# Lag of layer 2's output matmuls behind its features raised from 15 to 18, and the split of an early weight moved two steps later

## The chip, the cores and the metric

One NeuronCore of one Trainium2 chip runs the whole program. The metric is device time in microseconds (us) of one execution; three executions of the kernel before gave 966.13, 966.22 and 969.75 us, median 966.22.

## What is computed

Random-feature attention (4 x 8 heads, 576 positions, head size 64, 128 features), then two feed-forward layers on its 2304 x 512 result, all in fp32 accuracy:

```python
h = proj - sq; h = h - np.max(h, axis=-1, keepdims=True)
phi = np.exp(h) / np.sqrt(m)                       # of q and of k
num = einsum(q_p, k_p^T v);  den = einsum(q_p, sum k_p) + 1e-6
x = num / den                                      # attention, 2304 x 512
xn = x / rms * rms_g                               # layer 1, d_ff 1536
x = (silu(xn @ w_gate) * (xn @ w_val)) @ w_out
h = x @ w_in                                       # layer 2, d_ff 2048
out = (h * np.cos(h)) @ w_out
```

## The kernel before, in words

**Arithmetic.** A 32-bit operand of a feed-forward product is held as two parts, a high one (a ScalarE cast) and a low one (the difference, on GpSimd or VectorE), and a product is three matmuls: high x high, low x high, high x low. Layer 2's first product, and most of layer 1's, are done by a scheme that needs seven block products instead of eight (`PRODUCTS`).

**Weights (class `Weights`, L129).** A weight chunk of 128 x 512 numbers arrives as 64-bit floats (`load`, L160, a 512 KB transfer) and is made in two generators. `front` (L187) has six steps: (1) a shift on VectorE, (2) for some chunks a sign step on VectorE, (3) a mask on VectorE, (4) `exponent` of the next chunk, an ACTIVATE on ScalarE (L182 or L184) that reads the next chunk's raw tile, (5) a multiply-add on VectorE (L204), (6) the sum on GpSimd (L209). For the twelve early chunks the second generator is `early_back` (L329): its first step is the high cast on ScalarE (L214, `w<-f`) and the issue, on ScalarE's queue, of the load of the raw tile three chunks on; its second step is the low difference on GpSimd (L217). `run` (L314) takes steps of `front(c)` and `early_back(c - 1)` in turn: F1 B1 F2 B2 F3 F4 F5 F6. All engines take their instructions in the order in which this code writes them.

**Attention (L800 to L811).** 24 slots. Each projects one tile of keys or queries (`project`, L419, two PSUM banks of the pool "w", which has four), takes the largest entry on VectorE (L435, `kmx`, `qmx`), and eight exponentials on ScalarE (L437, `ke`, `qe`), four for each bank. Some slots also take a bank of the same pool for a transposition (L502). At the end of a slot `wts.tick` makes weight steps: five in slots 1 to 5, one in slots 6 to 13, four in slots 14 to 22. Eight steps make a chunk, so a chunk is two slots late in the stage.

**Layer 2 (L1182 to L1396).** 24 periods k: three pairs of token blocks by eight groups of two feature tiles. A period has seven `hidden(k, i)` products (six matmuls of 384 columns, L1043, banks `Xh` and `Yh`), each read out by a ScalarE copy (L1196; i = 0, 2, 3, 6) or a VectorE addition (L1199; i = 1, 4, 5). The next product into the same bank, two products on, waits for that. `cosine` (L1210) turns the sums into features: range reduction on VectorE (L1220, L1221), two ScalarE functions (L1017), a product on VectorE (L1232), a high cast on ScalarE (L1051) and a low difference on VectorE (L1054, `o<-turns,o`). `out2(k)` (L1236) is the output product of period k: 36 matmuls of 512 columns (L1251, `o_ps`), four slots of nine (three row blocks by three parts); they are written between the hidden products, `share[i]` of them behind product i. The list for k = 1 opens with fewer, and what it leaves out is the lag: 21 of 36 at k = 1, so 15 are left at each later period's start and run at its head. After each hidden product and after each share, `unit()` runs what is due: features, evictions, weight steps (1.3 back steps a unit), transfers.

A run is a stretch of periods with the same pair; its outputs stay in six PSUM banks and are evicted (L1282 a ScalarE copy, L1276 a VectorE addition) at matmuls 21, 24, 27, 30, 33 and 36 of the run's last `out2`. Runs open at k = 0, 3, 6, 12, 15, 20 and 22. Twenty weight tiles rotate (`RING`); `room` (L360) stops the back steps until `freed_by(k - 1)` (L1346) has told that the tiles of an earlier period have been read. Followed through the code, `room` stops the back steps of layer 2 only until the calls in periods 7 and 16; after the first the tiles of the second group follow one another at fixed distances (a chunk asked from memory is used eight units later), after the second those of the third.

Of the kernel before, what the change touches and what calls it, by code (L numbers as in the profile page):

```python
# [56 lines left out]
def attention_then_ffn(ctx: ExitStack, tc: tile.TileContext, qT, kT, v, omT, wc1, rms_g, wc2, out, B, H, S, D):  # L57
# [69 lines left out]
    class Weights:  # L127
# [186 lines left out]
        def run(self):  # L314

            self.exponent(0)
            yield
            for c in range(self.fused + 1):
                both = [self.front(c)] if c < self.fused else []
                if c > 0:  # L320
                    both.append(self.early_back(c - 1))
                while both:
                    for g in list(both):
                        if next(g, DONE) is DONE:
                            both.remove(g)
                        else:
                            yield
# [217 lines left out]
    with tc.manual_schedule():  # L545
# [467 lines left out]
        def unit():  # L1013
            now = due.setdefault(clock[0], [])
            while now:
                f, args = now.pop(0)
                f(*args)  # L1017
            del due[clock[0]]
            flush(1)
            wts.now += 1  # L1020
            wts.pace(*tempo)
            job(2 if clock[0] % 5 < 2 else 1)
            clock[0] += 1
# [150 lines left out]
        begins_run = [k == 0 or ends_run[k - 1] for k in range(NPER)]  # L1174
# [7 lines left out]
        def hidden(k, i):  # L1182

            n, g, p, fq = periods[k]
            f = 2 * fq
            which, name, acc = PRODUCTS[i]
            if i == 0:
                for x in "XY" if k % 2 == 0 else "YX":
                    banks2[k, x] = bank("wa", f"{x}h_{k}")[:, :NB]
            o = banks2[k, acc]  # L1190
            seventh(o, 2, p, f, which, name, i in (0, 1, 3))
            if i in (0, 2, 3, 6):
                if i in (2, 6) or (k, i) == (0, 0):
                    rows2[k + (i > 2), i // 2 % 3] = two_rows(F32, f"h{i}_{k}")
                a = rows2[k, 1][:, 3 - i] if i in (2, 3) else rows2[k + (i > 2), 0][:, int(i == 0)]
                nc.scalar.copy(a, o)  # L1196
            else:
                a = rows2[k, int(i > 1)][:, (1, 0, 1)[(1, 4, 5).index(i)]]
                nc.vector.tensor_tensor(a, o, a, op=ALU.add)  # L1199
            if i == 1:  # L1200
                cosine(k, rows2.pop((k, 0)), ([(k - 1, 2 * periods[k - 1][3] + 1, 2 * periods[k - 1][2])] if k else [])
                       + [(k, f, 2 * p)])
            elif k + 1 == NPER and i in (4, 5, 6):
                cosine(k, rows2[k + (i == 6), int(i < 6)], [(k, f + (i != 5), 2 * p + (i < 6))], int(i == 5))
            elif i == 5:
                cosine(k, rows2.pop((k, 1)), [(k, f + 1, 2 * p + 1), (k, f, 2 * p + 1)])
            if ends_run[k] and k + 1 < NPER:
                at(1, bring, 3 + periods[k + 1][1], periods[k + 1][2], name)
# [59 lines left out]
        def ask_sums(k):  # L1268
            for m, (blk, j) in enumerate([(2 * periods[k][2] + 1 - c, j) for c in range(2) for j in range(TPB)]):
                if (blk, j) in spilled:  # L1270
                    at(2 * m, ask_sum, blk, j)
# [74 lines left out]
        def freed_by(k):  # L1346

            n, g, p, fq = periods[k]
            if n + 1 == len(sessions) or sessions[n + 1][0] != g:
                wts.freed = first_tile[g] + sum(PARTS2[:GROUPS2[g].index(fq)]) + 3  # L1350
            elif sessions[n - 1][0] != g and fq == GROUPS2[g][0]:
                wts.freed = first_tile[g]
# [3 lines left out]
        for k in range(1, NPER):  # L1356
            loading = ends_run[k]
            tempo[:] = wts.rate(wts.fused + FRONT_GOALS[k], 14) if k in FRONT_GOALS else 0.0, 0.5 if loading else 1.3
            if ends_run[k - 1]:
                ask_sums(k - 1)  # L1360
            share = [1, 2, 3, 3, 4, 4, 4] if k == 1 else [5, 5, 3, 5, 6, 6, 6] if begins_run[k - 1] else [5, 5, 5, 5, 5, 5, 6]
            for i in range(7):
                if (k, i) == (len(GROUPS2[0]), 4):
                    assert not whole
                    wider.pop()
                    extra.close()
                    outs.append(ctx.enter_context(tc.tile_pool(name="outs", bufs=1, reuse_waits="tile")))
                hidden(k, i)
                unit()
                for _ in range(share[i]):  # L1370
                    next(o)
                unit()
                if i == 2 and k > 1:
                    freed_by(k - 1)
                if (i, k + 1) == (3, NPER):
                    ask_sums(k)
# [53 lines left out]
```

## Time and profile before

| | |
|---|---|
| median of three executions | 966.22 us |
| the profiled execution | 965.95 us, span 964.2 us |
| matmul (PE) busy | 951.0 us, 99% of the span |
| VectorE, ScalarE, GpSimd busy | 710.2, 537.1, 415.5 us |
| granted TensorE clock | 1.00 in the mean |
| DMA | 227.65 MB, mean 236 GB/s |

PE is TensorE's matmul row, DVE VectorE, ACT ScalarE, POOL GpSimd, SP the sync engine's queue. Times in rows are us from the span's start. In a row of a timeline the first number is the start, the second the length; `x16` counts the merged instructions, and the bracket gives idle time of that engine just before and who ended it. A projection or a kv product of four heads and two halves shows as 16 matmul records.

### The profile page before, as it was taken

What the parts mean: (1) busy time and instruction counts of PE and PEld (TensorE: products, weight loads), DVE (VectorE), ACT (ScalarE), POOL (GpSimd) and SP (SyncE); (2) the same over time, 40 slices, a digit from 0 to 9 for tenths busy, and PEclk for the clock granted to TensorE, in tenths of its full rate; (3) what the DMA queues carried; (4) which work ended last, traced back from release to release, by engine and by line L of the source; (5) the groups of instructions that cost most, each with busy time, mean ns of one, the idle gap of its engine ahead of it and who ended that gap; (6) DMA issues with size and microseconds to landing.
All of it is one profiled execution on the core that took longest, in us unless ns stands there. A gap on an engine that the chain in (4) does not pass through costs nothing. (4 is left out here: it accounts for less than half of the span.)

```text
span 964.2 us, 16225 instructions
## 1 busy us (share of the span) xinstructions
PE 951.0 (99%) x5761; PEld 894.6 (93%) x5761; DVE 710.2 (74%) x1163; ACT 537.1 (56%) x1155; POOL 415.5 (43%) x377
## 2 busy tenths in 40 slices
PE   9999999999999999999999999999999999999998
PEld 8998999989999999999999998889889889889997
DVE  5786677778863686577685758996799777785766
ACT  7787776775543524355443545575655565464443
POOL 2133366657944867275764663320244220130000
PEclk9999999999999999999999999999999999999999
DMA  8565187778697898856989794967622768307554
GB/s 311 159 179 186 56 279 277 253 267 261 220 329 289 331 331 290 302 154 196 391 281 370 263 356 142 352 226 262 207 88 85 265 199 293 120 23 264 203 219 166
DMA packets 96082, 227.65 MB, mean 236 GB/s; under 512 B 9728, under 2 KB 45184, under 8 KB 96000
## 3 DMA queue, kind: packets, MB, share of 16 engines
q1 hardware_dynamic: 94704, 222.34, 67.0%
q10 hardware_dynamic: 1296, 4.26, 1.3%
q8 instruction: 46, 0.75, 0.3%
q14 instruction: 36, 0.29, 0.1%
HBM read 156.04 MB, written 70.52 MB: 235 GB/s over the span
## 5 line engine op out<-in xcount | busy, mean ns | idle before, releaser
L1251 PE MATMUL o_ps<-w,o 128*128 128x512 f32 x864 | 225.7, 393 | 0.7 <-DVE o L1054 0.7
L209 POOL TENSOR_TENSOR f<-f,raw 128x512 f32<-128x512 f32 x68 | 94.3, 1387 | 234.9 <-DVE raw L204 205.1
L1251 PEld LDWEIGHTS o_ps<-w,o 128*128 128x128 f32 x864 | 159.6, 188 | 25.0 <-DVE o L1054 1.1
L217 POOL TENSOR_TENSOR w<-b,w 128x512 fp32r<-128x512 f32 x88 | 115.3, 1316 | 136.7 <-ACT w L214 127.0
L831 PE MATMUL gv_ps<-xhl,w 128*128 128x384 f32 x576 | 108.0, 335 | 1.6 <-DVE gv L870 1.1
L831 PEld LDWEIGHTS gv_ps<-xhl,w 128*128 128x128 f32 x576 | 100.6, 188 | 2.2 <-DVE gv L870 1.4
L1150 PE MATMUL y<-t,w 128*128 128x384 f32 x576 | 102.1, 334 | 0.3 <-POOL w L217 0.3
L1150 PEld LDWEIGHTS y<-t,w 128*128 128x128 f32 x576 | 100.0, 188 | 0.6 <-POOL w L217 0.6
L1051 ACT CAST o<-turns 128x384 fp32r<-128x384 f32 x96 | 47.5, 513 | 95.0 <-DVE turns L1232 95.0
L1043 PE MATMUL Xh<-T,w 128*128 128x384 f32 x432 | 88.6, 340 | 1.7 <-ACT h L1196 1.7
L1043 PEld LDWEIGHTS Xh<-T,w 128*128 128x128 f32 x432 | 78.0, 188 | 9.2 <-ACT h L1196 4.0
L1043 PE MATMUL X<-T,w 128*128 128x384 f32 x432 | 80.9, 335 | 0.0
L1043 PEld LDWEIGHTS X<-T,w 128*128 128x128 f32 x432 | 75.3, 188 | 0.3 <-DVE r L1078 0.2
L214 ACT CAST w<-b 128x512 fp32r<-128x512 f32 x88 | 50.5, 580 | 32.2 <-DVE b L274 25.1
L1054 DVE TENSOR_TENSOR o<-turns,o 128x384 fp32r<-128x384 f32 x96 | 59.9, 640 | 8.2 <-ACT o L1051 8.1
L884 PE MATMUL y_ps<-t,w 128*128 128x384 f32 x288 | 60.7, 346 | 0.0
L1043 PE MATMUL Yh<-B,w 128*128 128x384 f32 x288 | 58.7, 338 | 0.0
L1199 DVE TENSOR_TENSOR h<-Yh,h 128x384 f32<-128x384 f32 x48 | 26.6, 553 | 42.4 <-PE Yh L1043 41.5
L1221 DVE SCALAR_TENSOR_TENSOR turns<-turns,r 128x768 f32<-128x768 int32 (+1 forms) x50 | 56.4, 1128 | 1.7
L1017 ACT ACTIVATE turns<-turns,half_pi 128x768 f32<-128x768 f32 (+1 forms) x50 | 45.7, 915 | 21.4 <-DVE turns L1221 21.3
L190 DVE TENSOR_SCALAR f<-W 128x512 int32<-128x512 int32 x68 | 44.8, 658 | 15.2 <-ACT W L182 6.5
L1043 PEld LDWEIGHTS Yh<-B,w 128*128 128x128 f32 x288 | 52.2, 188 | 3.8 <-ACT h L1196 0.2
(117 smaller groups left out, 1882.0 us busy)
## 6 DMA issues: line engine op xcount, KB each, us to landing
T<-T_dram SPq DMA_DIRECT2D x48, 768.0 KB, 7.0
raw<-wc SPq DMA_DIRECT2D x60, 512.0 KB, 4.9
B<-yh_dram SPq DMA_DIRECT2D x21, 768.0 KB, 5.4
kept<-f SPq DMA_DIRECT2D x56, 256.0 KB, 4.8
b<-kept SPq DMA_DIRECT2D x56, 256.0 KB, 4.9
B<-x_dram SPq DMA_DIRECT2D x15, 768.0 KB, 6.9
x_dram<-xhl SPq DMA_DIRECT2D x12, 768.0 KB, 5.8
s<-x_dram SPq DMA_DIRECT2D x24, 384.0 KB, 5.9
```

Source lines behind the costliest of these rows:

```text
L209: nc.gpsimd.tensor_tensor(f32(f), f32(f), rest, op=ALU.add)
L214: nc.scalar.copy(t[:, 0, to], src)
L217: nc.gpsimd.tensor_tensor(t[:, 1, to], src, f32(t[:, 0, to]), op=ALU.subtract)
L831: nc.tensor.matmul(o, w[i], x[j], start=n == 0, stop=n == len(terms) - 1)
L884: nc.tensor.matmul(yacc[blk][e], w[:, i, e * P:(e + 1) * P], t[:, j], start=first and i + j == 0, stop=last and j == 1)
L1017: f(*args)
L1043: nc.tensor.matmul(o, w[:, i, c + kk * P:c + (kk + 1) * P], x[:, j, kk], start=begin and n == 0, stop=n == 5, skip_group_check=True)
L1051: nc.scalar.copy(t[:, 0], a)
L1054: engine.tensor_tensor(t[:, 1], a, f32(t[:, 0]), op=ALU.subtract)
L1150: nc.tensor.matmul(acc[e], w[:, i, e * P:(e + 1) * P], t[:, j], start=f == fs[0] and i + j == 0, stop=f == fs[-1] and j == 1)
L1221: nc.vector.scalar_tensor_tensor(r, a, -TWO_PI_LO, b, op0=ALU.mult, op1=ALU.add)
L1251: nc.tensor.matmul(oacc[blk][j], o[:, x, js], w[:, y], start=first and n == 0, stop=last and n == 2)
```

## The change

Two independent edits. In `run`, `early_back(c - 1)` joins two steps later, so the order of a chunk is F1 F2 F3 B1 F4 B2 F5 F6; no step is added or removed. In layer 2, the list for k = 1 gives 18 matmuls instead of 21, so every later period runs 18 of the previous `out2` before its own follows; `freed_by` is called one product later to match.

```diff
@@ run
             for c in range(self.fused + 1):
                 both = [self.front(c)] if c < self.fused else []
-                if c > 0:
-                    both.append(self.early_back(c - 1))
-                while both:
+                after = [self.early_back(c - 1)] if c > 0 else []
+                n = 0
+                while both or after:
+                    n += 1
+                    if n > 2 or not both:
+                        both += after
+                        after = []
                     for g in list(both):
@@ layer 2
-            share = [1, 2, 3, 3, 4, 4, 4] if k == 1 else [5, 5, 3, 5, 6, 6, 6] if begins_run[k - 1] else [5, 5, 5, 5, 5, 5, 6]
+            share = [0, 1, 2, 3, 3, 4, 5] if k == 1 else [5, 5, 3, 5, 6, 6, 6] if begins_run[k - 1] else [5, 5, 5, 5, 5, 5, 6]
@@
-                if i == 2 and k > 1:
+                if i == 3 and k > 1:
                     freed_by(k - 1)
```

## Rows read from the trace of the kernel before

**Rows 1.** The page, part 1: busy us, share of the span, instructions.

```profile
PE 951.0 (99%) x5761; PEld 894.6 (93%) x5761; DVE 710.2 (74%) x1163; ACT 537.1 (56%) x1155; POOL 415.5 (43%) x377
```

**Rows 2.** Who PE waited for, whole span: us in total, times, longest.

```profile
PE Xh L1043 <- ACT h L1196: 1.7, 3, 1.0
...
PE o_ps L1251 <- DVE o L1054: 0.7, 1, 0.7
```

**Rows 3.** Busy time by window, layer 2's periods 1, 2, 6 and 9 (start:end, length, busy).

```profile
585.15:599.48 14.33, 12.90 (x65) 10.94 (x64) 13.51 (x19) 8.02 (x16) 5.15 (x4) 1.00 0.07 25
599.48:617.03 17.55, 16.34 (x78) 14.00 (x79) 17.12 (x25) 11.47 (x24) 5.04 (x3) 1.00 0.87 285
...
664.64:680.40 15.76, 15.76 (x80) 14.19 (x79) 10.93 (x19) 7.78 (x13) 1.30 (x1) 1.00 0.57 186
...
711.87:727.60 15.73, 15.40 (x77) 13.62 (x76) 15.28 (x20) 9.02 (x17) 7.44 (x6) 1.00 0.31 104
```

**Rows 4.** Chain of work that ended last: the last 57 output matmuls.

```profile
947.55 12.98 PE o_ps L1251 x57
```

**Rows 5.** Timeline of PE, 76 to 86 us, around the project of slot 23.

```profile
82.90 0.48 PE L426 MATMUL qp_ps<-om,qraw 64*128 64x128 f32 x2
84.05 1.16 PE L426 MATMUL qp_ps<-om,qraw 64*128 64x128 f32 x14 [0.66 <-ACT ke L437]
85.13 1.98 PE L464 MATMUL num_ps<-kv,eT 128*64 128x128 f32 x32
```

**Rows 6.** Timelines of ACT, then DVE, slots 21 and 22.

```profile
81.08 0.64 ACT L452 COPY eT<-eT_ps 128x512 f32<-128x512 f32 x1
82.33 0.62 ACT L214 CAST w<-f 128x512 fp32r<-128x512 f32 x1 [0.62 <-POOL f L209]
...
82.86 2.17 ACT L437 ACTIVATE ke<-kp_ps,kmx 128x128 f32<-128x128 f32 x8
...
81.07 1.28 DVE L435 TENSOR_REDUCE kmx<-kp_ps 128x4 f32<-128x512 f32 x2
```

**Rows 7.** DMA view of 0 to 30 us (issues, KB, us to landing); timelines of ACT and PE.

```profile
raw<-wc SPq DMA_DIRECT2D x3, 512.0 KB, 6.8
raw<-wc ACTq DMA_DIRECT2D x3, 512.0 KB, 4.5
...
16.12 2.18 ACT L437 ACTIVATE ke<-kp_ps,kmx 128x128 f32<-128x128 f32 x8
...
21.22 2.29 ACT L437 ACTIVATE ke<-kp_ps,kmx 128x128 f32<-128x128 f32 x8
...
22.43 3.82 PE L587 MATMUL kv_ps<-v,ke 64*128 64x128 f32 x31
```

**Rows 8.** Timeline of PE, periods 1 and 2 of layer 2.

```profile
591.92 1.31 PE L1043 MATMUL Xh<-T,w 128*128 128x384 f32 x6 [0.31 <-ACT h L1196]
...
594.37 0.73 PE L1251 MATMUL o_ps<-w,o 128*128 128x512 f32 x2 [0.67 <-DVE o L1054]
...
599.48 1.31 PE L1043 MATMUL Xh<-B,w 128*128 128x384 f32 x6 [0.44 <-DVE h L1199]
...
610.05 1.31 PE L1043 MATMUL Xh<-T,w 128*128 128x384 f32 x6 [1.03 <-ACT h L1196]
```

**Rows 9.** Timeline of DVE in the same periods.

```profile
592.89 0.96 DVE L1221 SCALAR_TENSOR_TENSOR turns<-turns,r 128x768 f32<-128x768 int32 x1
...
598.88 0.54 DVE L1199 TENSOR_TENSOR h<-Yh,h 128x384 f32<-128x384 f32 x1
...
603.04 1.94 DVE L1221 SCALAR_TENSOR_TENSOR turns<-turns,r 128x768 f32<-128x768 int32 x1
```

**Rows 10.** Timelines of POOL at 600 us and of PE at 721 us.

```profile
600.51 3.65 POOL L217 TENSOR_TENSOR w<-b,w 128x512 fp32r<-128x512 f32 x2 [2.38 <-ACT w L214]
...
721.22 1.33 PE L1043 MATMUL Xh<-T,w 128*128 128x384 f32 x6 [0.33 <-ACT h L1196]
```

**Rows 11.** Costliest groups by line: the evictions of the output banks.

```profile
L1276 DVE TENSOR_TENSOR sum<-o_ps,sum 128x512 f32<-128x512 f32 x24 | 16.0, 685 | 5.3 <-PE o_ps L1251 5.3
```

## Prediction

> **What bounds the kernel now.** The order of views was: the page's busy times, the list of who PE waited for, the windows of layer 2, and then single timelines where PE stood still. The page gives PE 951.0 us busy of a span of 964.2 [rows 1]; neither edit adds or removes a matmul, so only the 13 us that PE isn't busy, and what lies hidden in its row, can change. The list of waits is short: thirteen lines of 1.7 us or less, the largest three copies by ACT of `Xh` and, of interest here, one wait of 0.7 us of an output matmul for its feature [rows 2]. The windows show where layer 2 loses time: period 6 takes 15.76 us with PE busy throughout, period 2 takes 17.55, and in periods 1 and 2 DVE is busy 13.51 of 14.33 and 17.12 of 17.55 us, against 10.93 of 15.76 in period 6 [rows 3]. So the kernel is bound by PE, save in a few places; the two that the edits touch are the start of layer 2, bound by DVE, and slots 20 to 23 of the attention.
>
> The profiled execution took 965.95 us, 0.27 below the median of 966.22; the sum is made against 965.95 and 0.27 is added at the end. A measurement of this kernel can tell about 0.5% (4.8 us) from no change.
>
> **Early weights: the gain.** In slot 23 PE makes two matmuls of a projection at 82.90 and the third only at 84.05; the next fourteen take 85.13 - 84.05 = 1.08 us, 0.077 each, so two should take 0.15 and 84.05 - 82.90 - 0.15 = 1.0 us is lost [rows 5]. The wait is for ACT's exponentials: a transposition took a bank before, so the second bank of this projection is the one that slot 22's first four exponentials read. They run from 82.86, half of 2.17 us, to 83.95. Their input was there early: DVE's maximum of the first bank ended at 81.07 + 0.64 = 81.71, and ACT's copy ahead of them at 81.72. What stands between is one cast of an early weight, which sat at the head of ACT's queue for 0.62 us until GpSimd's sum was made, and then took 0.62 [rows 6]. With the edit this cast is written one slot later, behind those exponentials and just ahead of the ACTIVATE of front step four. In the same way the cast of slot 19 comes to the end of slot 20; it can push slot 21's work on ACT by at most its own 0.62, so the exponentials of slot 22 start between 81.72 and 82.34, and four are done between 82.81 and 83.43, where PE asks at 83.05. That gives back 0.6 to 1.0; I take 0.8, and zero as the other end, if PE finds another wait right behind.
>
> **Early weights: the price.** `early_back` also issues a load on ACT's queue, so each load moves with its cast. From slot 14 on it has a whole chunk (two slots) to land. In the first slots ticks come five at a time: the load of chunk 3 moves from the end of slot 2 to the end of slot 3, while the ACTIVATE that reads it, the fifth step of chunk 2's list instead of the sixth, comes from the end of slot 5 to the end of slot 4, ahead of slot 5's exponentials. Slot 3's exponentials start at 16.12 and take 2.18 [rows 7]; without the cast of 0.62 ahead of them they end at about 17.7, and the load leaves then. Landing takes 4.5 us on this queue and 6.8 on SP's in the same 30 us [rows 7], so the tile is there at 22.2 or 24.5. With an ACTIVATE of about the cast's 0.62 the exponentials of slot 5 start at 22.8 or 25.1 instead of 21.22, and the first four end 1.1 later, at 23.9 or 26.2. PE wants them in the second half of its 31 kv matmuls, at 22.43 + 3.82/2 = 24.3 [rows 7]. So the price is 0 or 1.9; I take 0.2, since 4.5 is the row of the same queue and kind.
>
> The other moved instructions have one answer: the order within DVE's and GpSimd's queues stays as it was among the weight steps, and there are as many ticks, so from the fourth step of layer 1 on the program is the same.
>
> **The lag: periods 1 and 2.** An output matmul takes 12.98/57 = 0.228 us [rows 4]. Period 1 gets 0, 1, 2, 3, 3, 4, 5 in place of 1, 2, 3, 3, 4, 4, 4: three less, 0.68 us of PE work that ends up at the tail, where 54 in place of 51 matmuls follow the last product. Does PE reach the later products sooner in return? It waits at 591.92 for ACT's copy, at 594.37 for the low half of a feature, at 599.48 for DVE's addition, at 610.05 for ACT's copy again [rows 8]. The second wait goes: that matmul, the twelfth, then comes one hidden product later. The others stand in DVE's queue: the addition that 599.48 waits for runs at 598.88 [rows 9], in a window where DVE is busy 94% of the time [rows 3], and it depends on none of the deferred matmuls. PE then only arrives earlier and waits longer: 599.48 and 610.05 stay, and three matmuls fewer lie before them. I take +0.7. The other end is that PE's waits here all go: 14.33 - 12.90 = 1.4 in period 1 and 17.55 - 15.76 = 1.8 in period 2, together -3.2 [rows 3].
>
> **The lag: the room for weight tiles.** `freed_by` comes one product later, two units, 2 x 15.76/14 = 2.3 us. It is what the back steps wait for in periods 7 and 16. The second group's tiles follow one another at fixed distances from there, so their casts, additions and differences in periods 7 to 11 all come 2.3 us later; no tile is due that soon (the tightest, in period 11, is begun eight units, 9 us, ahead of its use, then seven). In period 9 PE stands 0.33 us at 721.22 for ACT's copy [rows 10]; a weight's cast is written just ahead of this copy and moves behind it. I take -0.3. The other end is one slow instruction more on DVE's path: a range reduction takes 0.96 us alone and 1.94 where GpSimd's differences (600.51 to 604.16) run beside it, so +1.0 [rows 9, 10]. By the Trainium skill (page SBUF — State Buffer, section Who interferes with whom) a VectorE instruction with two SBUF inputs and a GpSimd one that reads SBUF exclude each other for the whole of the first. The 1.94 beside 0.96 agrees. That rule speaks against moving the differences, and is the third rival.
>
> **The lag: evictions and tail.** At a run's end the banks are read at matmuls 21 to 36. With 18 left these fall one behind product 0, two behind product 1, one behind 2, and two (33 and 36) behind 3, where the fourth product had one before. VectorE's takes 0.685 [rows 11]. PE needs the addition of product 4 only at product 6, twelve matmuls (2.7 us) and a product later; two evictions take 1.4. So 0, with 6 run ends x 0.685 = 4.1 as the other end. The last six evictions and their transfers stand behind the same matmuls as before: 0.
>
> **Sum.** -0.8 + 0.2 + 0.7 - 0.3 = -0.2: 965.75 for the profiled execution, and with 0.27 **966.0 us**: no difference that can be told.
>
> **Rivals.**
> 1. *The lag frees PE* (0.12). If the waits of periods 1 and 2 hang on outputs being too close to their features, they go: 965.95 - 0.6 - 3.2 - 0.3 + 0.27 = 962.1, and more if later waits go too. For it: the wait at 594.37 is exactly this. Against it: DVE is over 94% busy there.
> 2. *The third raw tile is late* (0.09), on the other side. Place: the end of slot 4, where ACT stands at the ACTIVATE with slot 5's exponentials behind it and PE behind those. It decides from a landing after 22.6 (4.9 us); at 6.8 it costs 1.9 instead of 0.2: 967.7, slower than before.
> 3. *The moved differences meet VectorE's chain* (0.10): +1.0 in place of -0.3 in periods 7 to 11: 967.3.
> 4. *The paired evictions delay the read-out* (0.04): up to 4.1 more, 970.1.
> 5. *The edits don't reach PE* (0.03): the order changes only in work that is hidden, and the gap at 84 us is kept by DVE's maximum: 966.2.
>
> **How the numbers follow.** My forecast has 0.62. From 964.0 (the forecast with half of rival 1's gain) to 968.4 (rivals 2 and 3 together) lie the forecast, rivals 2, 3 and 5, and a part of rival 1; rival 4 and the rest are outside. Faster by over 0.5% (below 961.4) needs more than rival 1's whole 3.2, a third of its chance: 0.04. Slower by over 0.5% (above 971.1) needs rival 4 with another: 0.03. The rest, 0.93, is the same.
>
> **What would show it.** In the profile of the changed kernel: in slot 23 no wait of the projection for ACT (right), or the same 1.0 us with another releaser (wrong); ACT's ACTIVATE in slot 4 waiting for a transfer at about 21 to 22 us, and no gap of PE at 24 to 26; period 1 still some 14.3 us long with 18 output matmuls in it, the wait for a feature gone and longer waits for ACT and DVE in its place. If period 1 shrinks by more than 0.7 us, or period 2 ends earlier by the same count of matmuls, the reading of DVE as the bound there is wrong. If PE shows new waits for DVE behind products 3 to 6 of periods 4, 7, 13, 16, 21 and 23, rival 4 is right. A total outside 964.0 to 968.4 would make the prediction wrong.

## The result and the profile after

The changed kernel takes 976.46 us (median of six executions, 975.78 to 979.74) against 967.25 us for the kernel before beside it: a ratio of 1.0098, 95% interval 1.0079 to 1.0117. It is some 9 us slower, far above the forecast of 966.0 and outside its range. The profiled execution is the longest of the six (979.74 us, span 977.9). Lines of the code behind `run` are four higher than before (L1251 is L1255 now).

The page of the kernel after, the busy times of part 1 and the clock row of part 2; then the list of who PE waited for (total, times, longest, in us):

```profile
PE 958.2 (98%) x5761; PEld 898.9 (92%) x5761; DVE 713.6 (73%) x1163; ACT 536.0 (55%) x1155; POOL 418.2 (43%) x377
...
PEclk9899999999999999999999999999999999999999
```

```profile
PE Xh L1047 <- ACT h L1200: 2.0, 3, 1.0
PE kv_ps L591 <- DVE kv L602: 1.9, 2, 1.3
PE X L1047 <- DVE r L1082: 1.5, 1, 1.5
PE Xh L1047 <- DVE h L1203: 1.3, 3, 0.6
PE qp_ps L430 <- ACT ke L441: 1.3, 1, 1.3
```

The same 5761 matmuls are busy for 958.2 instead of 951.0 us [rows 1]. Waits are not in this number: the digit 8 in the clock row says that TensorE did not have its full clock in the second fortieth of the span. The wait of an output matmul for its feature [rows 2] is gone, as forecast; in its place stand two waits of the attention's kv product, a longer one of a projection (1.3 instead of 0.7), one of layer 1 (`X`, which the last section takes up), and more of layer 2's products.

**Where the time went.** The n-th matmul into a tile of one name is the same matmul in both kernels, so the difference of their starts is a running account. It stands at 0.2 us by 21 us, 1.8 at the first kv product behind 24 us, 5.1 behind this product at 31 us, 5.6 at 66, 6.5 at 77, 7.1 at 91, 8.7 at 96, 9.0 at 143, 10.7 at 370, 11.1 at the end of layer 2's period 2, 12.6 at 752 and 13.4 at the last matmul. Most of it is there before layer 2 begins. The account is 4 us above the difference of the medians, since the profiled execution is the longest: 1.6 us of it stand for a second fall of the clock at 92 us and 1.7 for a wait at 370 us; whether the other five executions have these isn't shown. PE's timeline of the kernel after, at the four steps in the attention:

```profile
24.13 7.25 PE L591 MATMUL kv_ps<-v,ke 64*128 64x128 f32 x32 [1.31 <-DVE kv L602]
...
66.11 1.16 PE L430 MATMUL kp_ps<-om,kraw 64*128 64x128 f32 x14 [0.58 <-ACT ke L441]
...
76.60 4.03 PE L591 MATMUL kv_ps<-v,ke 64*128 64x128 f32 x32 [0.58 <-DVE kv L602]
91.18 1.16 PE L430 MATMUL qp_ps<-om,qraw 64*128 64x128 f32 x14 [1.30 <-ACT ke L441]
```

The first kv product waits for VectorE's copy of the previous one, and then its 32 matmuls take 7.25 us where 31 took 3.82 [rows 7]. The windows of 22 to 32 us of the kernel after (busy times of PE, PEld, DVE, ACT and POOL, granted clock, DMA share, GB/s) say why:

```profile
22.00:24.00 2.00, 0.83 (x15) 0.63 (x11) 1.97 (x6) 1.67 (x6) 1.41 (x1) 1.00 0.80 243
24.00:26.00 2.00, 1.87 (x9) 1.87 (x10) 2.00 (x6) 1.37 (x7) 0.91 (x1) 0.59 0.59 221
26.00:28.00 2.00, 2.00 (x10) 1.78 (x9) 0.88 (x2) 2.00 (x8) 0.49 (x1) 0.50 0.04 12
28.00:30.00 2.00, 2.00 (x11) 2.00 (x11) 0.00 (x0) 0.15 (x1) 0.00 (x0) 0.50 0.50 131
30.00:32.00 2.00, 2.00 (x19) 1.84 (x20) 0.00 (x0) 0.00 (x0) 0.00 (x0) 0.70 0.00 0
```

PE is busy for 0.83 of the 2 us from 22 to 24, and then the granted clock is 0.50, the lower of the two levels (1.2 GHz), where the kernel before has 1.00 throughout. The gap itself costs 1.6 us of the account. The low clock behind it costs 3.3; by these windows it lasted 6.8 us. Behind the gap at 91 us the clock falls once more in this execution (0.66 and 0.50 from 92 to 96 us), for another 1.6.

**Why VectorE was late.** Its timeline, and below it GpSimd's, of the kernel after:

```profile
19.37 1.03 DVE L190 TENSOR_SCALAR f<-W 128x512 int32<-128x512 int32 x1 [0.92 <-ACT W L184]
20.43 1.66 DVE L193 SCALAR_TENSOR_TENSOR f<-W,f 128x512 int32<-128x512 int32 x1
22.12 0.43 DVE L195 TENSOR_SCALAR raw<-f 128x512 int32<-128x512 int32 x1
22.46 1.28 DVE L439 TENSOR_REDUCE kmx<-kp_ps 128x4 f32<-128x512 f32 x2
23.66 0.76 DVE L602 COPY kv<-kv_ps 128x260 f32<-128x260 f32 x2
```

```profile
18.84 1.27 POOL L217 TENSOR_TENSOR w<-f,w 128x512 fp32r<-128x512 f32 x1 [3.68 <-ACT w L214]
20.07 1.46 POOL L209 TENSOR_TENSOR f<-f,raw 128x512 f32<-128x512 f32 x1
```

The same steps in VectorE's and GpSimd's timelines of the kernel before:

```profile
18.88 0.45 DVE L190 TENSOR_SCALAR f<-W 128x512 int32<-128x512 int32 x1 [0.84 <-ACT W L184]
19.37 0.69 DVE L193 SCALAR_TENSOR_TENSOR f<-W,f 128x512 int32<-128x512 int32 x1
20.09 0.43 DVE L195 TENSOR_SCALAR raw<-f 128x512 int32<-128x512 int32 x1
20.44 1.28 DVE L435 TENSOR_REDUCE kmx<-kp_ps 128x4 f32<-128x512 f32 x2
21.64 0.75 DVE L598 COPY kv<-kv_ps 128x260 f32<-128x260 f32 x2
```

```profile
16.29 1.51 POOL L217 TENSOR_TENSOR w<-f,w 128x512 fp32r<-128x512 f32 x1 [0.73 <-DMA v<-v]
17.76 1.29 POOL L209 TENSOR_TENSOR f<-f,raw 128x512 f32<-128x512 f32 x1
```

A difference and a sum on GpSimd, which were done by 19.05 us before chunk 2's sign step began, now run beside its shift and its sign step: 1.03 instead of 0.45 and 1.66 instead of 0.69 us. The two maxima and the kv copies, in order behind them on VectorE, come two microseconds later. About 0.5 of the two is ScalarE's: the moved cast stands ahead of the ACTIVATE that chunk 2's shift waits for, and the shift begins at 19.37 instead of 18.88. The third raw tile was not late: the ACTIVATE in slot 4 waits 0.24 us for it, at 22.43.

Over the whole program the view of that one source line gives it (count, shortest, median and longest in ns, first and last start), before and after:

```profile
L193 DVE SCALAR_TENSOR_TENSOR f<-W,f x12: 678/786/1677, 19.4 to 357.5; 128x512 int32<-128x512 int32 x12
```

```profile
L193 DVE SCALAR_TENSOR_TENSOR f<-W,f x12: 691/1516/1678, 20.4 to 368.5; 128x512 int32<-128x512 int32 x12
```

The median doubled. One by one, the sign steps of the four early chunks (2, 5, 8 and 11) took 0.68 to 0.78 us before and take 1.66 to 1.68 now; the other eight, of later weights, are much as they were, and the 1.68 of the kernel before is one of those.

The gap at 91 us is of the same make: VectorE's and then GpSimd's timeline of the kernel after in slot 22:

```profile
87.69 1.66 DVE L193 SCALAR_TENSOR_TENSOR f<-W,f 128x512 int32<-128x512 int32 x1
89.27 1.28 DVE L439 TENSOR_REDUCE kmx<-kp_ps 128x4 f32<-128x512 f32 x2
```

```profile
87.40 1.41 POOL L209 TENSOR_TENSOR f<-f,raw 128x512 f32<-128x512 f32 x1 [0.82 <-DVE raw L204]
```

The sign step also moved a tick forward, ahead of the slot's maxima: the delayed back steps leave F1 F2 F3 at the head of a chunk's list, where it was F1 B1 F2 B2 F3.

### The profile page after: what moved, and what is told of

It is laid out like the page before. It is cut to its first block, busy times and chain, and to the rows that moved or that the text cites. A ratio compares the mean times of both kernels' runs of the same rounds, so it can differ in the third digit from the quotient of the medians.

```text
span 977.9 us, 16215 instructions
## 1 busy us (share of the span) xinstructions
PE 958.2 (98%) x5761; PEld 898.9 (92%) x5761; DVE 713.6 (73%) x1163; ACT 536.0 (55%) x1155; POOL 418.2 (43%) x377
## 5 line engine op out<-in xcount | busy, mean ns | idle before, releaser
L1255 PE MATMUL o_ps<-w,o 128*128 128x512 f32 x864 | 225.3, 393 | 0.0
L1255 PEld LDWEIGHTS o_ps<-w,o 128*128 128x128 f32 x864 | 159.7, 188 | 24.1
L217 POOL TENSOR_TENSOR w<-b,w 128x512 fp32r<-128x512 f32 x88 | 118.9, 1357 | 136.5 <-ACT w L214 118.6
L1047 PEld LDWEIGHTS Xh<-T,w 128*128 128x128 f32 x432 | 77.8, 188 | 10.7 <-ACT h L1200 4.3
L1058 DVE TENSOR_TENSOR o<-turns,o 128x384 fp32r<-128x384 f32 x96 | 56.8, 610 | 7.0 <-ACT o L1055 6.7
L1236 DVE TENSOR_TENSOR turns<-h,turns 128x768 f32<-128x768 f32 (+1 forms) x50 | 53.5, 1070 | 2.7 <-ACT turns L1021 2.5
```

Source lines behind the costliest of these rows:

```text
L217: nc.gpsimd.tensor_tensor(t[:, 1, to], src, f32(t[:, 0, to]), op=ALU.subtract)
L1047: nc.tensor.matmul(o, w[:, i, c + kk * P:c + (kk + 1) * P], x[:, j, kk], start=begin and n == 0, stop=n == 5, skip_group_check=True)
L1058: engine.tensor_tensor(t[:, 1], a, f32(t[:, 0]), op=ALU.subtract)
L1236: at(mu, lambda: nc.vector.tensor_tensor(r, h, r, op=ALU.mult))
L1255: nc.tensor.matmul(oacc[blk][j], o[:, x, js], w[:, y], start=first and n == 0, stop=last and n == 2)
```

## Experiments

All ratios are to the kernel before on the same chip, with 95% intervals; 0.001 is 0.97 us.

**The two edits apart.** The first run has the early edit alone, the second the lag (list and `freed_by`) alone.

```diff
@@ run: as in the change; layer 2 as before
```

> The early-weight edit alone, layer 2 as before. Theory A (GpSimd's moved sums and differences now run beside VectorE's sign step of chunks 2, 5 and 8, the maxima and the copies of the kv sums come late, PE stands for over 1 us at about 23 and 91 us, and its granted clock falls to half behind each such gap): most of the loss is here, +6 to +9 us, 973 to 976, with a window of clock 0.5 at 24 to 31 us. Theory B (the lag is what costs): within 1 us of the kernel before. Theory C (the third raw tile lands late): the loss is here as in A, but ACT waits for the transfer at 22 us for over 1 us.

Measured: 974.66 us, 1.0083 [1.0069, 1.0097]; the gap stands at 24.66 us (1.31, for the kv copy), with the low clock behind it. A second gap of the same length, where the expectation saw a low clock too, leaves it at 1.00:

```profile
91.68 1.16 PE L430 MATMUL qp_ps<-om,qraw 64*128 64x128 f32 x14 [1.31 <-ACT ke L441]
```

```diff
@@ layer 2: as in the change; run as before
```

> The lag and the later freed_by alone, the early weights as before. Theory A: only the three deferred matmuls and the moved weight train, +0.7 to +2 us, 968 to 969, clock 1.00 throughout. Theory B: +6 to +9 us, 973 to 976.

Measured: 969.16 us, 1.0032 [1.0020, 1.0043], just above the expected 968 to 969. In its profile the clock falls to 0.57 and 0.58 from 212 to 216 us, behind two waits of PE (0.91 at 210.20, 0.43 at 211.08) that the kernel before has too (0.90 and 0.42) and keeps its full clock after; the 1.5 us that this costs are given back at 224 us, where a wait of 1.08 of the kernel before is gone. So about 8 of the 9 us are the early edit and 3 or less the lag; together they make a little more than the change did.

**Does the sign step do it?** The early edit, with the sign step of early chunks in the third front step, behind the maxima again.

```diff
-            if not self.signed(c):
+            if not self.early and not self.signed(c):
                 (sign step)
             yield
+            if self.early and not self.signed(c):
+                (sign step)
```

> The early-weight edit alone, with VectorE's sign step of an early chunk made in its third front step instead of its second, so that it falls into the same slots as in the kernel before. Theory A: the gaps of PE at about 66 and 91 us go back to 0.5 us and less, the one at about 23 us stays (there the sign step is in slot 4 in all cases), with its half clock: +3 to +6 us, 970 to 973. If the sign step's place doesn't matter: the same as with the early edit alone.

Measured: 970.19 us, 1.0033 [1.0020, 1.0047]. VectorE's timeline of this run, chunks 2 and 8, and PE's at the second place:

```profile
21.22 1.66 DVE L196 SCALAR_TENSOR_TENSOR f<-W,f 128x512 int32<-128x512 int32 x1
...
87.41 0.68 DVE L196 SCALAR_TENSOR_TENSOR f<-W,f 128x512 int32<-128x512 int32 x1
```

```profile
88.05 1.23 PE L432 MATMUL qp_ps<-om,qraw 64*128 64x128 f32 x16
```

In slot 22 the step is 0.68 again and the projection of slot 23 runs its sixteen without a stop: the account falls by 1.06 there, from 5.14 ahead of the projection to 4.08 behind it, so the forecast gain of 0.8 exists. In slot 3 the step still meets GpSimd's sum (1.66), the gap of 1.30 at 24.93 stays, and the low clock with it.

**Only the later chunks delayed.** The early edit from chunk 4 on.

```diff
-                    if n > 2 or not both:
+                    if n > 2 or c < 4 or not both:
```

> The early-weight edit alone, but only from the fourth chunk's list on, so that slots 1 to 6 are as before. Theory A: no gap at 23 us and no half clock at 24 to 31 us; the gap at about 91 us (then about 86) stays, with or without a short half clock: 0 to +4 us, 967 to 971. Theory C gives the same for the first gap. If the loss came from the later slots alone: as with the early edit alone.

Measured: 969.01 us, 1.0021 [1.0012, 1.0030]. No gap at 23 us and the clock at 1.00 throughout: three quarters of the early edit's price (0.0062 of 0.0083) are the chunks 0 to 3. The gap at the projection of slot 23 is there (1.30 at 85.71), with the sign step at 82.21 taking 1.67 beside GpSimd's sum.

**Is GpSimd beside the sign step enough?** The kernel before, with two GpSimd products, on a part of a tile that is not yet in use, at the end of slot 3.

```diff
@@ ahead of the slots
+        nc.gpsimd.memset(kv[3][:, 0:512], 1.0)
@@ at the end of a slot, behind wts.tick
+            if s == 3:
+                for _ in range(2):
+                    nc.gpsimd.tensor_tensor(kv[3][:, 0:512], kv[3][:, 0:512], kv[3][:, 0:512], op=ALU.mult)
```

> The kernel before, with two GpSimd products of 128 x 512 on an unused tile behind slot 3's weight steps, so that GpSimd reads SBUF while VectorE makes chunk 2's shift and sign step in slot 4. Nothing else is moved. Theory A (VectorE's steps wait for GpSimd's instruction, the copies of the kv sums come late): the sign step takes over 1.3 us in place of 0.7, PE has a gap of 0.7 to 1.5 us at about 22 to 24 us, and where it is over 1 us a half clock follows: +1 to +6 us. Theory C (the gap came from the transfer or from ACT's order of the cast and the ACTIVATE): no gap, 967.

Measured: 969.43 us, 1.0029 [1.0019, 1.0039]. VectorE's, GpSimd's and PE's timelines of this run:

```profile
19.69 1.41 DVE L193 SCALAR_TENSOR_TENSOR f<-W,f 128x512 int32<-128x512 int32 x1
21.13 1.15 DVE L195 TENSOR_SCALAR raw<-f 128x512 int32<-128x512 int32 x1
```

```profile
19.33 2.67 POOL L815 TENSOR_TENSOR kv<-kv 128x512 f32<-128x512 f32 x2
```

```profile
23.86 5.25 PE L587 MATMUL kv_ps<-v,ke 64*128 64x128 f32 x32 [0.96 <-DVE kv L598]
```

Nothing of the order was changed, and yet sign step and mask together take 2.56 instead of 0.69 + 0.43 = 1.12 us, PE waits for the kv copy, and the clock falls (0.61 and 0.54 from 26 to 30 us). By the account the gap costs 1.2 and the low clock 1.7. GpSimd's work beside these steps is enough for the gap and for the low clock (here behind 0.96, where the expectation had asked for over 1 us), though not for the whole price of the early edit.

**Or is lateness alone enough?** The kernel before, with slot 5's second maximum taken twice, and in the other run four times.

```diff
+            for _ in range(2 if (nm, t, r) == ("k", 5, 1) else 1):
                 (the maximum)
```

> The kernel before, with slot 5's second maximum made twice (0.64 us more on VectorE ahead of the copies of the kv sums). PE's gap at 22 us is then about 0.4 us. If a gap costs its own length: +0.4, 967.4, and the clock stays at 1.00. If any gap here brings the half clock: +4 us.

> The kernel before, with slot 5's second maximum made four times (1.9 us more on VectorE). PE's gap at 22 us is then about 1.6 us. If a gap costs its own length: +1.6, 968.6. Theory A (behind a gap of this size the granted clock is half for 3.4 to 6.8 us, in which PE does half of its work): +4 to +6 us, 971 to 973, with no other change in the program.

Measured: 967.35 us, 1.0004 [0.9995, 1.0013] with one more; 970.77 us, 1.0041 [1.0027, 1.0055] with three more. PE's timeline of the one and of the other:

```profile
23.03 4.03 PE L588 MATMUL kv_ps<-v,ke 64*128 64x128 f32 x32 [0.25 <-DVE kv L599]
```

```profile
24.75 5.62 PE L588 MATMUL kv_ps<-v,ke 64*128 64x128 f32 x32 [1.69 <-DVE kv L599]
```

A gap that costs 0.5 us of the account moves the time by less than can be told, and the 32 matmuls take their full-clock 4.03 us. With two maxima more on top they take 5.62, at a granted clock of 0.50 from 28 to 30 us: 2.0 us of the account for the gap and 1.7 for the clock. So at this place of the program it is the gap that brings the clock down, whoever made it, and the price is not proportional to it. Elsewhere a gap of that length need not: 1.31 at 91.68 us with the early edit alone and 1.30 at 85.71 with the later chunks delayed left the clock at 1.00, where 1.30 at 91.18 in the change brought it down.

**The lag taken apart.** First `freed_by` one product later in the kernel before, then the list alone.

```diff
-                if i == 2 and k > 1:
+                if i == 3 and k > 1:
```

> The kernel before, with only the call of freed_by one product later; lag 15. Theory A (the lag costs 0.7 us by its three deferred matmuls, and the rest of its 2.2 us by the weight train of periods 7 to 11 coming two units later): +1 to +1.5 us, 968 to 968.5, with new waits of PE for VectorE and ACT in periods 9 to 11 and none in periods 1 and 2. Theory B (the freed tiles cost nothing, the whole 2.2 us is the deferral in periods 1 and 2 and at the run ends): 967 as before.

Measured: 969.11 us, 1.0024 [1.0015, 1.0033]. PE's timeline from 715 to 745 us; the one wait of the kernel before there is that at 721.22 [rows 10]:

```profile
716.97 1.32 PE L1043 MATMUL Xh<-T,w 128*128 128x384 f32 x6 [0.34 <-ACT h L1196]
729.09 1.33 PE L1043 MATMUL Xh<-B,w 128*128 128x384 f32 x6 [0.21 <-DVE h L1199]
740.99 1.31 PE L1043 MATMUL Yh<-B,w 128*128 128x384 f32 x6 [0.28 <-ACT h L1196]
```

The time is above the expected 968 to 968.5. The wait at 721.22 is gone, and the account falls by 0.6 there, for the 0.3 forecast; but the weight steps that moved off it made three others, and between 716 and 742 us 1.6 us is lost on balance.

```diff
-            share = [1, 2, 3, 3, 4, 4, 4] if k == 1 else
+            share = [0, 1, 2, 3, 3, 4, 5] if k == 1 else
```

> The kernel before with the list of period 1 changed to 0, 1, 2, 3, 3, 4, 5 (lag 18), and freed_by where it was. By my theory the lag's price has two parts, 0.7 us of deferred matmuls and 1.8 us of shifted weight steps, and only the first is left here: +0.7, the waits in periods 9 to 11 as in the kernel before. If the price is that of the lag itself (outputs farther behind, evictions paired) it stays at the +2.2 that both parts of the lag showed together.

Measured: 967.74 us, 1.0008 [0.9998, 1.0018], and in its profile the last matmul is 0.80 us later than before (0.18 of it from ahead of period 1), with PE's only wait between 715 and 770 us the old one (0.32, at 721.35). The median can't be told from no change, but in the profile the list costs the 0.7 of the forecast, within a tenth; the rest of the lag's price is `freed_by`.

**The early edit mended.** Chunks 0 to 3 as before, the sign step of the later ones in the third front step.

```diff
-                    if n > 2 or not both:
+                    if n > 2 or c < 4 or not both:
@@ front: the sign step in the third step where self.early and c >= 4
```

> The kernel before with the early edit from chunk 4 on only, and with the sign step of chunks 4 and later in the third front step. My theory: what is wrong with the early edit is where it puts GpSimd's work beside VectorE's sign step and ahead of the maxima, at 23 us and at 91 us; what was forecast of it at slot 23 (-0.8) is real. So with chunks 0 to 3 as before there is no gap at 23 us, with the sign step moved none at 91 us, PE's 0.66 us wait at 84 us is gone, and the offset to the kernel before is between -0.9 and +0.2 us by 100 us: 965.5 to 966.7 for a kernel before of 966.5. The rival, that the moved loads or casts cost something by themselves wherever they stand, keeps the +1.7 us by 90 us that the delay from chunk 4 on showed alone: 968 to 969.

Measured: 967.07 us, 1.0000 [0.9989, 1.0010]. PE's timeline:

```profile
71.53 4.03 PE L593 MATMUL kv_ps<-v,ke 64*128 64x128 f32 x32 [0.58 <-DVE kv L604]
...
84.31 1.24 PE L432 MATMUL qp_ps<-om,qraw 64*128 64x128 f32 x16
```

Both large gaps are gone, and so is the 0.66 wait of slot 23 [rows 5]: the account falls by 1.07 us there. A new wait for a kv copy at 71.53, with a short one ahead of it, had taken 0.9 before, so the edit in this form is worth nothing. VectorE's timeline of this run shows where that wait comes from:

```profile
66.69 1.76 DVE L498 SCALAR_TENSOR_TENSOR x<-x,ms,gain 128x512 f32<-128x512 f32 x1 [0.72 <-POOL ms L494]
```

The moved difference now stands in GpSimd's queue ahead of a small step of the attention (`ms`), and VectorE waits 0.72 us for that step, with the maxima and the kv copy behind it. The change has the same wait (0.71 at 71.77), ahead of its kv product at 76.60.

**Less lag instead of more.** The list of the kernel before with 24 instead of 21 output matmuls in period 1, by itself, and in one run with the mended early edit.

```diff
-            share = [1, 2, 3, 3, 4, 4, 4] if k == 1 else
+            share = [1, 2, 3, 3, 4, 5, 6] if k == 1 else
```

> The kernel before with the lag at 12: period 1 has 1, 2, 3, 3, 4, 5, 6. The mirror of the share alone: by my theory -0.7, since periods 1 and 2 end when VectorE lets them and three more matmuls fit before that end; by the rival, outputs too close to their features, 0 to +0.5, with more waits of output matmuls for VectorE's low halves.

> The run e9 with the lag at 12 instead of 15 (period 1 runs 24 of its output matmuls in place of 21), freed_by as before. If VectorE alone sets the ends of periods 1 and 2, as forecast, three more output matmuls fit in PE's waits there and 0.7 us leaves the tail: 0.7 below e9. The rival is that outputs closer to their features wait for them: the wait of 0.67 us of an output matmul in period 1 comes several times, and the time is that of e9 or 0.5 above it.

Measured: 965.75 us, 0.9996 [0.9987, 1.0004] alone; 966.56 us, 0.9998 [0.9989, 1.0007] with the other. The sign is that of the forecast, but neither can be told from no change. In the two profiles the account does fall by 0.7 between layer 2's period 1 and the last matmul, as expected of three matmuls fewer at the tail. None of the versions beats the kernel before by what a measurement can tell.

## Why the prediction was wrong, point by point

**The step that failed** is the one sentence on the queues: "The other moved instructions have one answer: the order within DVE's and GpSimd's queues stays as it was among the weight steps". The order among the weight steps within each queue did stay. Three other things moved. GpSimd's queue shifted against VectorE's, so that its differences and sums run beside the shift and the sign step; this costs 0.6 to 1.0 us a time, as the kernel after and the GpSimd run show. And the sign step moved against the maxima of the attention on VectorE, which the sign-step run shows at slot 22. And a difference moved ahead of the attention's own step on GpSimd, as the mended version shows at 66.69 us. The rival that named this meeting (the third) put it in layer 2 alone, at +1.0; the view of that one source line of the kernel before (678/786/1677) would have shown what such a step can take: 0.68 to 0.78 us for the early weights and up to 1.68 for later ones. By the Trainium skill (page SBUF — State Buffer, section Who interferes with whom) a VectorE instruction with two SBUF inputs contends with a GpSimd one that reads SBUF, and a `tensor_scalar` can do so in a two-port mode; the trace agrees for both (0.69 and 1.66, 0.45 and 1.03 us).

**What made 1.6 us into 4.9** stands in no term of the sum: the granted clock. The kernel before has it at 1.00, so each gap of PE was priced at its own length; its waits of 0.90 and 0.42 at 210 us and of 1.08 at 224 us had cost no clock. The runs with a gap at 23 us show 1.7 to 3.3 us on top where the gap itself cost 1.2 to 2.0 of the account, and nothing where it cost 0.5.

**Right, as far as it went:** the wait at 84 us. It does give back 1.06 or 1.07 us where the sign step is out of the way, for the 0.8 forecast (0.6 to 1.0). In the change itself the maximum took the cast's place in front of the exponentials, with 1.30 us instead of 0.66. The third raw tile: 0.24 us of waiting, and rival 2 falls. **The price of 0 to 1.9 for the early edit** was thus made for the wrong resource, a transfer; the edit costs 8.0 by its ratio.

**The lag in periods 1 and 2** went as forecast. PE's timeline of the kernel after there:

```profile
603.04 1.31 PE L1047 MATMUL Xh<-T,w 128*128 128x384 f32 x6 [0.64 <-ACT h L1200]
607.55 1.31 PE L1047 MATMUL Xh<-T,w 128*128 128x384 f32 x6 [0.51 <-DVE h L1203]
610.58 1.31 PE L1047 MATMUL Xh<-B,w 128*128 128x384 f32 x6 [0.57 <-DVE h L1203]
621.16 1.31 PE L1047 MATMUL Xh<-T,w 128*128 128x384 f32 x6 [1.02 <-ACT h L1200]
```

The first, third and last answer to 591.92, 599.48 and 610.05 [rows 8], the first two of these longer now; the one at 607.55 is new, the output matmul's wait is gone, and the account is the same behind the stretch as ahead of it (11.1). Rival 1 falls. The evictions cost nothing that a wait shows.

**The room for weight tiles** was mis-sized: the wait at 721.22 did go, but the same shift made three new waits, and the term is +1.6 us by the account (+1.4 to +3.2 by the run's interval) where the forecast's other end was +1.0. The three stand in the kernel after too:

```profile
727.89 1.32 PE L1047 MATMUL Xh<-T,w 128*128 128x384 f32 x6 [0.34 <-ACT h L1200]
740.02 1.32 PE L1047 MATMUL Xh<-B,w 128*128 128x384 f32 x6 [0.23 <-DVE h L1203]
751.92 1.33 PE L1047 MATMUL Yh<-B,w 128*128 128x384 f32 x6 [0.29 <-ACT h L1200]
```

**The sum with the measured terms:** 8.0 for the early edit (by its ratio), 0.8 for the list and 1.6 for `freed_by` (by the accounts) make 10.4, for 9.2 between the medians; the difference is within what the intervals of the single runs leave. The upper end of the range was added wrongly as well: rivals 2 and 3 stand 1.7 and 1.3 above the forecast, and together make 969.0, not 968.4; the result lies far above either.

**Open.** Behind the gap at 23 us the low clock costs twice as much in the change and in the early edit alone (3.3 us of the account each) as in the other three runs (1.7) because it lasts twice as long, 6.8 instead of 3.4 us; why it does is open. So is why a like gap brings the clock down in one place or execution and not in another. The 0.5 us of the cast ahead of the ACTIVATE was not tried by itself, nor was a change of the chunks 0 and 1 without GpSimd's differences.

## What to carry to other kernels

A step that moves in one engine's queue moves against all the others: list what now runs beside each of VectorE's two-input steps, and what of the main work stands in the queue behind them, before a move is called free. Price a gap of PE not by its length alone: a gap of about a microsecond can cost as much again, or twice that, in clock, and it can cost nothing more. How busy PE is around it did not tell which: in the change PE was busy 0.82 of the 2 us from 90 to 92 and the clock fell; with the early edit alone it was busy 0.69 of the same 2 us and the clock stayed. So look at the granted clock behind the gap, and give the forecast both prices. And where one wait goes because work was shifted in time, ask of each later product what the shifted work now meets, not only of the one that was helped.

## What the runs showed of the hardware that was not expected

A gap of 0.96 us reported at PE (1.2 of the account) was enough for the granted clock to fall to 0.5, and the 32 kv matmuls behind it took 5.25 instead of 4.03 us; after a reported gap of 0.25 there it stayed at 1.00. It also stayed at 1.00 after the longest wait of all the profiles, 1.72 us at 369.25 in the run with the early edit alone. The Trainium skill (page TensorE: Matmul & The Clock Gate, section Part 1: The HAM clock gate) tells of the half-rate state as that of an idle engine; here the longest wait just ahead of a fall was 1.69 us, and the measurement decides.

A wait of PE of 1.49 us in layer 1 (the longest of the kernel after, at 370 us) looks like a part of the change, but the same product waits in the run with less lag too (0.67 us at 360.97), whose code up to there is that of the kernel before. The two runs with the mended early edit, the same code up to there, have 1.16 us and none; the runs with the sign step moved and with the later chunks delayed have none. So it comes and goes without an edit; whether the full early edit makes it longer (1.49 and 1.72) isn't shown. VectorE's timeline of the run with less lag alone, and GpSimd's:

```profile
357.71 1.32 DVE L190 TENSOR_SCALAR f<-W 128x512 int32<-128x512 int32 x1 [0.34 <-DMA kept<-f]
```

```profile
357.44 1.30 POOL L209 TENSOR_TENSOR f<-f,raw 128x512 f32<-128x512 f32 x1 [2.76 <-DVE raw L204]
```

The shift waited 0.34 us for a transfer, so GpSimd's sum began first, and the shift then took 1.32 us; in the list-only run it began 0.1 us ahead of the sum and took 0.43. In these two runs the one that begins first keeps its time and the other pays, and the landing of a transfer decided which began first.
